# One ring of five buffers for k's results, in place of a ring of three and one of two

## The chip, the cores and the metric

The kernel runs on one core of a Trainium2 chip. The metric is the device time of one execution in microseconds (us), as the median of several runs. Of a profiled execution, the trace gives the times of all instructions from the start of its span.

## The reference

Two branches read the same `x` (2048 tokens, width 640, float32) and are mixed by a gate per token. Branch `a` is linear attention with 32 heads of 20, branch `b` a gated unit with 1536 inner columns.

```
phi = lambda t: jnp.where(t > 0, t + 1, jnp.exp(t)) + 1e-6
q, k, v = split(x @ wqkv)                       # per head
pq, pk = phi(q), phi(k)
kv = einsum("bhsd,bhse->bhde", pk, v)           # sum over tokens
z  = einsum("bhsd->bhd", pk)                    # sum of phi(k) over tokens
o  = (pq @ kv) / (pq . z + 1e-6)
a  = o @ wo
b  = (sigmoid(x @ w_gate) * (x @ w_up)) @ w_down
g  = sigmoid((x * gate_w).sum(-1, keepdims=True))
out = g * a + (1 - g) * b
```

The change touches only the part that computes `phi(k)` and `z`.

## The kernel before

All products are float32, each split into a high and a low part and made of three matmuls (`mm3`, lines 406 to 408). In the first stage (about the first 140 us) the kernel makes `phi(k)` for all tokens and at once multiplies it with the tokens' rows of `x`, into `gt`. The other stages (queries, the gated unit, the output) follow and do not use the tiles of this change.

The tokens stand in 16 tiles of 128. A block `b` (0 to 7) is a pair of token tiles, side 0 from one half of the tokens and side 1 from the other. Four chunks of two blocks each are worked off. Blocks 0 and 1 (`KPlain`) use plain products. Blocks 2 to 7 (`KBlock`) use a scheme with fewer products: seven of them (`s1` to `s7`), of which sums and differences, formed ahead on VectorE (DVE), are the operands. For each chunk the steps of both its blocks alternate: `s1` of a, `s1` of b, ... `s5` of b, and then `s6`, `s7`, `sum_b` and `phi` of each. Between these products PE works on `GTBatch` parts, the products of `phi(k)` and `x` of earlier blocks.

A block has two results of 640 columns (and two columns for the gate):

- side 0 is finished by `phi_a`: ScalarE (ACT) applies Exp and Relu to sums in `ta` and PSUM, the Relu parts go to a new tile `kr` (320 columns used, 320 wide), and DVE combines them.
- side 1 is collected in a tile `kb` (two halves of 322 columns), which `s3` allocates and ACT and DVE fill in `s3`, `s5` and `sum_b`; `phi_b` then works in place. In `KPlain`, `phi_b` allocates `kb` itself.

Either result `r` then has two readers. `z_add(r)` issues a DMA on GpSimd's (POOL's) queue that adds the tile to `zacc` (`accum_op`); each such DMA writes all of `zacc`. `k_split` (ACT and DVE) makes the high and the low part, `pkh` and `pkl`. Only when all these have read the tile can its buffer be given to a later tile of the same ring; the wait for that stands at the later tile's first writer. Rings are made by the tile pool `p1`, by tag: tag `kr` has three buffers, tag `kb` two.

The order of instructions is written out by the kernel's own planner (`Order`). It keeps a clock for PE, ACT and DVE, and puts queued work (splits of `x`, sums, weight splits) between the fixed steps wherever by these clocks it fits (`fill`, `_fits`). `place` finds, for a tile, the tile that had its buffer before, by the tag's number of buffers, and `data` takes the end of that tile's last use into account. `Ring` and `Rings` do the same for the two DMA queues, with the contiguous run of both sides of a transfer (`Ring.run`) as a term of its length. On the chip each engine runs its instructions in the order written, and waits by semaphores.

PE's products accumulate in PSUM tiles `ch`, `dd`, `cc` and `rot`. A block's `s3`, `s5` and `s6` all go to its `ch`: `s5` may start only when ACT has copied `s3`'s sum from `ch` to `kb[:, 0]`, and `s6` when ACT has copied `s5`'s to `kb[:, 1]`.

Of the kernel before, what the change touches and what calls it, by code (L numbers as in the profile page):

```python
# [7 lines left out]
F32 = mybir.dt.float32  # L8
# [6 lines left out]
P = 128  # L15
# [6 lines left out]
HALF = D // 2  # L22
HW = HALF + 2
# [350 lines left out]
def gated_mix_kernel(ctx: ExitStack, tc: tile.TileContext, xt, xn, wk, wv, wo, wst_q, wst_f, out_t):  # L374
# [38 lines left out]
    def prod(out, terms, first):  # L413
        for n, t in enumerate(terms):
            mm3(out, *t, first and n == 0, n == len(terms) - 1)

    def act(out, src, fn, after="", **kw):
        order.on_act(width(out), after, out, src)
        nc.scalar.activation(out, src, fn, **kw)  # L419
# [5 lines left out]
    def vec3(out, a, scalar, b, op0, op1, after=""):  # L425
        order.on_vec(width(out), after, 1.0, out, a, b)
        nc.vector.scalar_tensor_tensor(out, a, scalar, b, op0=op0, op1=op1)
# [57 lines left out]
    p1 = p1_cm.__enter__()  # L485
# [291 lines left out]
    def tok(b, side):  # L777

        pr, j = divmod(b, 4)
        return (2 * pr + side) * 4 + j  # L780
# [18 lines left out]
    def phi(dst, lo_src, hi_src, i):  # L799

        e = m1.tile([P, 2, HALF], F32, name="ke", tag="ma", bufs=2)
        act(e[:, 0], lo_src[:, :HALF], AF.Exp, "pv")
        act(e[:, 1], hi_src[:, :HALF], AF.Exp)
        act(dst[:, 0], lo_src[:, :HALF], AF.Relu)
        act(dst[:, 1], hi_src[:, :HALF], AF.Relu)
        vec_copy(logit[:, i:i + 1], lo_src[:, HALF:HALF + 1])
        vec3(dst, e, 1.0, dst, OP.min, OP.add, "a")
        KR[i] = dst
        z_add(dst)

    def vec_copy(out, src, after=""):
        order.on_vec(width(out), after, 1.0, out, src)
        nc.vector.tensor_copy(out, src)

    def kr_tile():
        return p1.tile([P, 2, HALF], F32, name="kr", tag="kr", bufs=3)

    class KBlock:
        def __init__(self, b):
# [23 lines left out]

        def s3(self):
            order.need(("pk", self.b - 2))
            self.kb = p1.tile([P, 2, HW], F32, name="kb", tag="kb", bufs=2)
            prod(self.ch[:, :HW], self.xt(1, ksh[:, 1], ksl[:, 1]), False)
            act(self.kb[:, 0], self.ch[:, :HW], AF.Copy, "p")

# [21 lines left out]
            add(self.kb[:, 0], self.cc[:, :HW], self.kb[:, 0], "p")  # L871

        def phi_a(self):
            phi(kr_tile(), self.ta, self.ch, tok(self.b, 0))

        def phi_b(self):
            i = tok(self.b, 1)
            e = m1.tile([P, 2, HALF], F32, name="ke", tag="ma", bufs=2)
            k = self.kb[:, :, :HALF]
            act(e, k, AF.Exp, "pv")  # L880
            vec_copy(logit[:, i:i + 1], self.kb[:, 0, HALF:HALF + 1])
            act(k, k, AF.Relu)
            vec3(k, e, 1.0, k, OP.min, OP.add, "a")
            KR[i] = k
            z_add(k)

    class KPlain:
# [15 lines left out]
                    mm3(self.ps[s][h][:, :HW], *x, *k_half(k, h), k == 0, k == KC - 1)  # L903

        def phi_a(self):
            phi(kr_tile(), *self.ps[0], tok(self.b, 0))

        def phi_b(self):
            kb = p1.tile([P, 2, HW], F32, name="kb", tag="kb", bufs=2)
            phi(kb[:, :, :HALF], *self.ps[1], tok(self.b, 1))  # L910

    def k_split(i, after=""):
# [14 lines left out]
    def z_add(r):  # L927

        gp.dma_start(zacc.rearrange(view2, j=2), r, accum_op=OP.add if z_started else OP.bypass)
        z_started.append(1)  # L930
# [1675 lines left out]
```

## Time and profile before

| | us |
|---|---|
| median of 3 runs | 732.84 (732.79 to 733.18) |
| the profiled execution | 732.54 |
| its span, first to last instruction | 730.6 |
| PE busy in the span | 724.0 |
| DVE busy | 563.7 |
| ACT busy | 360.1 |
| POOL busy | 94.7 |

A row of a timeline gives the start, the duration, the engine, the line of the program, the operation, and out<-in by the names of the tiles; a bracket at its end gives the idle time of the engine before it and what ended it. Most instructions come from helpers, so that many share a line (L419 is ACT's helper, L423 that of DVE for two tensors, L363 the one that issues DMAs); they are told apart by their tiles. "PE ch L406 <- ACT kb" reads: a matmul into `ch` waited for an ACT instruction on `kb`.

### The profile page before, as it was taken

The page shows a single profiled execution, that of the slowest core. Times are in us where ns is not written, and L with a number is a line of the kernel's source. Part 1 is how long each engine was busy: PE and PEld are TensorE (multiplying, and loading weights), DVE is VectorE, ACT ScalarE, POOL GpSimd, SP SyncE. Part 2 cuts the span into 40 slices and gives each one's busy share as a digit, 9 for nine tenths or more (in the row PEclk, how much of TensorE's full clock was granted, in tenths as well). Part 3 has the DMA queues.
Part 4 walks back from the last instruction along what each step waited for, and adds up shares of the span by engine and source line. Part 5 has one row for each costly group of instructions (what it writes and reads, how often), then busy time and mean ns, then how long its engine had stood idle before and what let it go on. Part 6 is the DMA issues. An engine that isn't in the chain of part 4 may idle for free.

```text
span 730.6 us, 10105 instructions
## 1 busy us (share of the span) xinstructions
PE 724.0 (99%) x3569; PEld 622.0 (85%) x3569; DVE 563.7 (77%) x989; ACT 360.1 (49%) x668; POOL 94.7 (13%) x161
## 2 busy tenths in 40 slices
PE   9989999999999999999999999999999999999997
PEld 8989999988888888888888888888888888888886
DVE  6878787987777889898989973457585867698783
ACT  6864648357556653535455363454333232334550
POOL 0211111113221211111210032001000041000000
PEclk9999999999999999999999999999999999999999
DMA  7655648698787866457687389879889697859212
GB/s 248 168 166 118 186 108 243 152 347 295 273 296 258 330 241 237 185 212 256 255 324 265 106 295 333 310 247 316 253 286 340 211 326 213 298 217 340 83 62 102
DMA packets 71945, 173.54 MB, mean 238 GB/s; under 512 B 11690, under 2 KB 33466, under 8 KB 68310
## 3 DMA queue, kind: packets, MB, share of 16 engines
q1 hardware_dynamic: 55526, 109.99, 46.2%
q0 software_dynamic: 16224, 62.74, 24.2%
q8 instruction: 28, 0.46, 0.2%
q14 instruction: 23, 0.19, 0.1%
q10 hardware_dynamic: 144, 0.16, 0.1%
HBM read 103.96 MB, written 63.92 MB: 230 GB/s over the span
## 4 chain that ended last, share of the span: by engine, by line
PE 98%; DMA 1%; DVE 1%; ACT 0%; issue 0%; ACTq 0%
PE ch L406 11%; PE ch L408 10%; PE ch L407 10%; PE cc L408 9%; PE cc L406 9%; PE cc L407 9%; PE dd L406 7%; PE dd L408 7%; PE dd L407 7%; PE rot L408 6%; PE rot L407 6%; PE rot L406 6%; PE rot L1505 1%; DMA zacc<-kb 1%; PE rot L494 0%; PE ch L980 0%
## 5 line engine op out<-in xcount | busy, mean ns | idle before, releaser
L419 ACT ACTIVATE c<-ch 128x512 f32<-128x512 f32 x52 | 31.1, 598 | 96.4 <-PE ch L408 96.2
L423 DVE TENSOR_TENSOR hf<-c,hf 128x512 fp32r<-128x512 f32 x75 | 51.1, 686 | 24.7 <-ACT hf L419 24.5
L419 ACT ACTIVATE hf<-c 128x512 fp32r<-128x512 f32 x75 | 46.0, 624 | 28.0 <-DVE c L423 28.0
L423 DVE TENSOR_TENSOR c<-cc,c 128x512 f32<-128x512 f32 x40 | 27.6, 689 | 37.6 <-PE cc L408 24.3
L406 PE MATMUL ch<-xth,ws 128*128 128x512 f32 x112 | 43.7, 390 | 0.0
L407 PE MATMUL ch<-xtl,ws 128*128 128x512 f32 x112 | 43.6, 389 | 0.0
L408 PE MATMUL ch<-xth,ws 128*128 128x512 f32 x112 | 43.6, 389 | 0.0
L423 DVE TENSOR_TENSOR tb<-rot,tb 128x512 f32<-128x512 f32 (+1 forms) x61 | 39.2, 672 | 3.0 <-PE rot L408 3.0
L423 DVE TENSOR_TENSOR tb<-dd,tb 128x512 f32<-128x512 f32 x44 | 30.1, 685 | 9.7 <-PE dd L408 9.6
L406 PE MATMUL dd<-xrh,wg 128*128 128x512 f32 x90 | 35.2, 391 | 0.0
L408 PE MATMUL dd<-xrh,wg 128*128 128x512 f32 x90 | 35.0, 389 | 0.0
L407 PE MATMUL dd<-xrl,wg 128*128 128x512 f32 x90 | 35.0, 389 | 0.0
L419 ACT ACTIVATE c<-dd 128x512 f32<-128x512 f32 x22 | 13.1, 598 | 44.2 <-PE dd L408 44.2
L423 DVE TENSOR_TENSOR c<-c,c 128x512 f32<-128x512 f32 x46 | 31.6, 686 | 2.6 <-ACT c L419 2.0
L406 PE MATMUL cc<-xbh,ws 128*128 128x512 f32 x84 | 32.7, 389 | 0.0
L407 PE MATMUL cc<-xbl,ws 128*128 128x512 f32 x84 | 32.7, 389 | 0.0
L408 PE MATMUL cc<-xbh,ws 128*128 128x512 f32 x84 | 32.7, 389 | 0.0
L419 ACT ACTIVATE dd<-ch 128x512 f32<-128x512 f32 x22 | 12.8, 582 | 33.6 <-PE ch L408 33.6
L423 DVE TENSOR_TENSOR wst<-wst 128x256 f32<-128x256 f32 (+2 forms) x69 | 27.4, 412 | 1.4
L408 PEld LDWEIGHTS ch<-xth,ws 128*128 128x128 f32 x112 | 21.0, 188 | 4.7 <-DVE ws L423 0.3
L407 PEld LDWEIGHTS ch<-xtl,ws 128*128 128x128 f32 x112 | 21.0, 188 | 4.3
L406 PEld LDWEIGHTS ch<-xth,ws 128*128 128x128 f32 x112 | 21.0, 188 | 4.1
(643 smaller groups left out, 2349.8 us busy)
## 6 DMA issues: line engine op xcount, KB each, us to landing
wf<-ws POOLq DMA_DIRECT2D x12, 1152.0 KB, 7.7
ws<-wf SPq DMA_DIRECT2D x11, 1152.0 KB, 8.1
wst<-wst_f SPq DMA_DIRECT2D x12, 640.0 KB, 5.2
wf<-wg POOLq DMA_DIRECT2D x12, 640.0 KB, 6.2
wd<-wd POOLq DMA_DIRECT2D x12, 640.0 KB, 8.1
wg<-wf SPq DMA_DIRECT2D x12, 640.0 KB, 5.3
wf<-wd SPq DMA_DIRECT2D x10, 640.0 KB, 9.2
xnst<-xn SPq DMA_DIRECT2D x16, 320.0 KB, 4.3
```

Source lines behind the costliest of these rows:

```text
L406: nc.tensor.matmul(out, l_hi, r_hi, start=first, stop=False, skip_group_check=True)
L407: nc.tensor.matmul(out, l_hi, r_lo, start=False, stop=False, skip_group_check=True)
L408: nc.tensor.matmul(out, l_lo, r_hi, start=False, stop=last, skip_group_check=True)
L419: nc.scalar.activation(out, src, fn, **kw)
L423: nc.vector.tensor_tensor(out, a, b, op=op)
L1505: nc.tensor.matmul(ps[:w, :w], v[:, m, :w], gt[:, m, c0:c0 + w], start=(m == 0), stop=(m == KC - 1))
```

## The change

`kr_tile` now makes tiles of the width of `kb` under one tag with five buffers, and `kb` tiles are made by it too. `phi_a` uses 320 of the 322 columns of each half, so that a `kr` tile is no longer one contiguous row in its partition.

```
-    def kr_tile():
-        return p1.tile([P, 2, HALF], F32, name="kr", tag="kr", bufs=3)
+    def kr_tile(name="kr"):
+        return p1.tile([P, 2, HW], F32, name=name, tag="kr", bufs=5)
...
     # KBlock.s3
-            self.kb = p1.tile([P, 2, HW], F32, name="kb", tag="kb", bufs=2)
+            self.kb = kr_tile("kb")
...
     # KBlock.phi_a
-            phi(kr_tile(), self.ta, self.ch, tok(self.b, 0))
+            phi(kr_tile()[:, :, :HALF], self.ta, self.ch, tok(self.b, 0))
...
     # KPlain.phi_a
-            phi(kr_tile(), *self.ps[0], tok(self.b, 0))
+            phi(kr_tile()[:, :, :HALF], *self.ps[0], tok(self.b, 0))
...
     # KPlain.phi_b
-            kb = p1.tile([P, 2, HW], F32, name="kb", tag="kb", bufs=2)
+            kb = kr_tile("kb")
             phi(kb[:, :, :HALF], *self.ps[1], tok(self.b, 1))
```

## The prediction

> **What bounds the kernel now.** I read the page first, for the busy shares and the chain that ended last.
>
> ```profile
> span 730.6 us, 10105 instructions
> PE 724.0 (99%) x3569; PEld 622.0 (85%) x3569; DVE 563.7 (77%) x989; ACT 360.1 (49%) x668; POOL 94.7 (13%) x161
> PE 98%; DMA 1%; DVE 1%; ACT 0%; issue 0%; ACTq 0%
> PE ch L406 11%; PE ch L408 10%; PE ch L407 10%; PE cc L408 9%; PE cc L406 9%; PE cc L407 9%; PE dd L406 7%; PE dd L408 7%; PE dd L407 7%; PE rot L408 6%; PE rot L407 6%; PE rot L406 6%; PE rot L1505 1%; DMA zacc<-kb 1%; PE rot L494 0%; PE ch L980 0%
> ```
>
> PE is the bound: 98% of the chain is matmuls. A change of buffers can only move the remaining 2%. In that rest one entry is not compute: `DMA zacc<-kb`, the accumulation into `zacc` that reads a `kb` tile, which is a tile of this change. So the next view is who PE waited for, over the whole span.
>
> ```profile
> PE ch L406 <- ACT kb L419: 2.0, 2, 1.2
> PE rot L494 <- PEq L2597: 0.8, 1, 0.8
> ```
>
> That is all of it: 0.8 us at the warm-up, and two waits of 2.0 us together for ACT writing `kb`. Where they are, the table by stretches shows.
>
> ```profile
> 36.00:41.00 5.00, 5.00 (x36) 5.00 (x34) 4.46 (x10) 1.17 (x3) 1.21 (x1) 1.00 0.34 53
> 41.00:45.00 4.00, 1.99 (x12) 1.47 (x12) 2.00 (x5) 3.00 (x8) 0.00 (x0) 1.00 0.11 17
> 45.00:49.00 4.00, 4.00 (x29) 4.00 (x29) 4.00 (x8) 3.62 (x8) 0.00 (x0) 1.00 0.95 295
> ```
>
> The first busy column after the length is PE. Before 41 us and after 45 us it is full; between them it has 1.99 of 4.00 us, 12 matmuls in place of 29. This is the first block pair that uses the transformed products (blocks 2 and 3). The reason is in ACT's timeline and in the chain of waits (its row for the DMA follows here last).
>
> ```profile
> 37.17 0.62 ACT L419 ACTIVATE xth<-xst 128x512 fp32r<-128x512 f32 x1
> 42.00 0.44 ACT L419 ACTIVATE kb<-ch 128x322 f32<-128x322 f32 x1 [4.20 <-DMA zacc<-kb]
> 42.34 0.62 ACT L419 ACTIVATE xth<-xst 128x512 fp32r<-128x512 f32 x1
> 42.86 0.46 ACT L419 ACTIVATE ksh<-xnl 128x322 fp32r<-128x322 f32 x1
> 43.58 0.46 ACT L419 ACTIVATE k5h<-pkl 128x322 fp32r<-128x322 f32 x1
> 43.95 0.76 ACT L419 ACTIVATE kb<-ch 128x322 f32<-128x322 f32 x2
> ...
> 37.77 4.13 DMA zacc<-kb
> ```
>
> At 42.00 ACT evicts block 3's product into its new `kb` tile. The ring has two `kb` buffers; block 3 gets the one of block 1, which the accumulation issued at 37.77 still reads until 41.90. ACT stands still for 4.20 us, and behind it are queued the split of `xth`, the weight splits and the next two evictions.
>
> **The change part by part.** (1) The wait goes. In the order of allocation (`kr0 kb0 kr1 kb1 kb2 kb3 kr2 kr3 kb4 kb5 kr4 kr5 ...`) `kb3` is the sixth tile, so in a ring of five it takes the buffer of `kr0`; it is also the first buffer given back. Its accumulation is long over:
>
> ```profile
> 18.89 0.68 POOL L363 DMA_DIRECT2D zacc<-kr  x1 [18.37 <-DVE logit L813]
> 23.23 1.26 POOL L363 DMA_DIRECT2D zacc<-kb  x1 [3.67 <-DVE logit L813]
> ```
>
> Each accumulation waits for the one before it to land, since all write `zacc`; so `kr0` is free at 23.23 at the latest, 14 us before ACT wants it. What the wait costs PE:
>
> ```profile
> 37.53 0.30 PE L406 MATMUL cc<-ksh,xth 128*128 128x322 f32 x1
> 40.96 0.30 PE L408 MATMUL ch<-ksh,xtl 128*128 128x322 f32 x1
> 42.50 0.41 PE L406 MATMUL ch<-ksh,xth 128*128 128x322 f32 x1 [1.23 <-ACT kb L419]
> 43.33 0.31 PE L408 MATMUL ch<-ksh,xtl 128*128 128x322 f32 x1
> 44.42 0.42 PE L406 MATMUL ch<-k2h,xth 128*128 128x322 f32 x1 [0.78 <-ACT kb L419]
> 44.83 0.30 PE L408 MATMUL ch<-k2h,xtl 128*128 128x322 f32 x1
> ```
>
> From 37.53 to 40.96 PE starts 24 matmuls, 23 steps of 3.43 / 23 = 0.149 us. From 40.96 to 44.83 it makes 9 steps (six of block 3's `s5`, then three of block 2's `s6`), which undisturbed are 9 x 0.149 = 1.34 us and took 3.87. Lost: 2.53 us. That is more than the 2.0 of the waits view, because the first matmul after each gap also takes 0.41 and 0.42 instead of 0.30.
>
> (2) Is something else late there? With the wait gone, ACT evicts `kb3` at 37.8 (end of `xth` at 37.79). The second gap (0.78) comes from ACT's queue: block 2's next eviction stands behind `xth` and three weight splits, whose inputs DVE makes:
>
> ```profile
> 38.56 0.68 DVE L423 TENSOR_TENSOR xst<-xst 128x512 f32<-128x512 f32 x1
> 39.98 0.49 DVE L423 TENSOR_TENSOR pkl<-pkl 128x322 f32<-128x322 f32 x1
> 43.00 0.69 DVE L423 TENSOR_TENSOR xtl<-xst,xth 128x512 fp32r<-128x512 f32 x1 [2.53 <-ACT xth L419]
> 44.82 0.88 DVE L423 TENSOR_TENSOR kb<-cc,kb 128x322 f32<-128x322 f32 x2
> ```
>
> `xth` can start when its sum ends, 38.56 + 0.68 = 39.24; with ACT's own steps (0.52 to the first `ksh`) the last split `k5h` waits for its sum, 39.98 + 0.49 = 40.47, and runs to about 40.9. Block 2's eviction then needs PE's `s5`, which ends at 40.96 + 0.30 = 41.26; it runs to 41.7. PE reaches `s6` at 40.96 + 7 x 0.149 = 42.00. So this gap closes too, with 0.3 us to spare. On DVE the stretch from `xtl` to the two `kb` sums (1.82 us from 43.00 to 44.82) moves to begin at 40.47; the first sum ends near 42.8, and `s7`, which needs it, starts at 42.00 + 9 x 0.149 = 43.34: 0.5 us to spare. If my chain through ACT is wrong by more than these 0.3, the second gap stays (0.78 and its slow matmul, 44.42 - 43.33 - 0.15 = 0.94): gain 2.53 - 0.94 = 1.59. Ends: 1.59 and 2.53; I take 2.53, since every step of the upper one has its row.
>
> (3) The other rings. Every later tile now also takes a buffer with another history. By allocation five back, the tightest are `kr4` after `kb3` and `kr6` after `kb5`:
>
> ```profile
> 64.58 1.18 POOL L363 DMA_DIRECT2D zacc<-kb  x1 [3.58 <-DVE xst L423]
> 97.08 1.19 POOL L363 DMA_DIRECT2D zacc<-kb  x1 [3.32 <-DVE xst L423]
> 80.60 0.47 ACT L419 ACTIVATE kr<-ta 128x320 f32<-128x320 f32 x1
> 114.40 0.46 ACT L419 ACTIVATE kr<-ta 128x320 f32<-128x320 f32 x1
> ```
>
> With the slowest landing of a `kb` accumulation (8.0, below) they are free at 72.6 and 105.1, 8 and 9 us before they are written. No new wait: 0.
>
> (4) `kr` tiles become as wide as `kb` tiles, and only 320 of 322 columns are used, so their accumulation reads two runs per partition instead of one. The `kb` tiles have that form already, so their rows price it.
>
> ```profile
> L363 POOL DMA_DIRECT2D zacc<-kr x8: 678/888/922, 18.9 to 132.0; - x8
> DMA to landing us min/median/max: 3.6/4.1/8.6
> L363 POOL DMA_DIRECT2D zacc<-kb x8: 1183/1192/1265, 23.2 to 136.1; - x8
> DMA to landing us min/median/max: 4.1/4.4/8.0
> L432 DVE TENSOR_SCALAR zperm<-zacc x1: 814/814/814, 180.3 to 180.3; 128x640 f32<-128x640 f32 x1
> ```
>
> Each of eight `kr` accumulations costs POOL 1.19 instead of 0.89 us and lands 0.3 later by the medians. What hides it: with the ring wait gone, the next reader of `zacc` is the copy at 180.3, over 40 us behind the last issue at 136.1. Taken at 0; if the chain of accumulations stood on the path, 8 x 0.30 = 2.4 us.
>
> The Trainium skill speaks against this edit: its page "Perfetto Trace Analysis", section "Contiguity and DMAs", says that for DMA it is contiguity within a partition line that matters, and wants layouts to keep it; here a contiguous 640 becomes 320 + 320. The rows agree in sign, with 0.30 us of POOL and 0.3 of landing; by the rule alone the time would not fall, by the rows the loss is behind a 40 us cover.
>
> (5) The order of instructions comes from the planner, which knows the rings (it looks up a tile's predecessor by the number of buffers) and the run lengths. In its own clocks no ring wait of `kr` or `kb` binds, before or with the new predecessors, so these lookups change nothing. The shorter run makes its `kr` transfers a little longer and their share of the engines smaller; worked through by its formulas this moves a store of `qp` by some hundredths of a us, less than the closest of the decisions that follow it. I take the order as unchanged.
>
> Sum: 2.53 + 0 + 0 + 0. From 44.83 on PE has no further wait in the view, so all that follows moves forward by the same amount. The profiled execution took 732.54 us (span 730.6 and 1.9 around it) and becomes 730.0. It lies 0.3 below the median of the runs (732.84), so for the median I say 730.3. A measurement of this kernel can tell 0.2%, 1.5 us, from no change.
>
> **Rivals.** (a) The wait goes and another takes part of its place: ACT's or DVE's queue is late at `s6` or `s7`. For it: spare time of only 0.3 and 0.5 us; against: each input has its row. Gain 1.0 to 1.6, so 731.2 to 731.8. 10%, half of it beyond 0.2%.
>
> (b) The longer `kr` accumulations stand on a path after all: 2.53 - 2.4 leaves 0.1, 732.7. Against: 8 us of margin at the tightest buffer and 40 at `zacc`. 3%. The contiguity rule of the Trainium skill ("Perfetto Trace Analysis", "Contiguity and DMAs") points this way.
>
> (c) The change does not do what it says: `kb3` gets a buffer whose accumulation is as late as now. For it: only that the pool, not the kernel, picks the buffer; against: at that point four of the five are either unused or returned earlier. 732.8, 3%.
>
> (d) Slower: the planner's order does change somewhere in chunks 2 and 3, and an ACT instruction is put in front of an eviction that PE needs. It decides once that instruction (0.44 to 0.62 us by the rows of ACT) is longer than the eviction's lead over PE, about 0.3 us at `s6`. Price, from the nearest rows: a gap such as the one here, 2.53; one in each of the two later chunks gives 730.3 + 5.06 = 735.4. Against: (5). 8%.
>
> **How the numbers follow.** The forecast has 76%, alone from 729.8 to 731.1. Taking in (a) up to its weaker end and the uncertainty of the runs, the range is 729.8 to 732.2; (b), (c) and (d), 14%, are mostly outside. Faster by over 0.2%: 76 + 5 = 81%. Within 0.2%: 5 + 3 + 3 = 11%. Slower: 8%.
>
> **What would show it.** Right: PE's waits have no entry for ACT `kb`; ACT evicts `kb` twice within about 1 us near 37 to 38; PE is full between 41 and 45 us; `zacc<-kb` leaves the chain; POOL's issue for `kr` is near 1.19 us; instruction counts are unchanged and DVE's `zperm` starts near 177.8. Wrong in step 2: a PE wait at 42 to 43 us with ACT or DVE as releaser. Wrong in step 3: an ACT wait for `zacc<-kr` or `zacc<-kb` at 70 to 120. Wrong in step 5: other instructions next to each other on ACT and DVE, and new waits of PE after 45 us.

## The result, and the profile after

| | before | changed |
|---|---|---|
| median, us (9 runs each) | 732.22 (730.82 to 733.18) | 730.48 (730.01 to 730.97) |
| the profiled execution | 732.54 | 730.48 |
| its span | 730.6 | 728.6 |

The ratio is 0.9976, with a 95% interval of 0.9966 to 0.9986: faster by 0.24%, between 0.14 and 0.34%. The forecast, 730.3 us, is 0.2 off the measured median; as a change it was 2.53 us, or 0.35%, and the measured 1.74 us between the medians is less. Why it is less is the question of the experiments.

First the page of the changed kernel (busy times, and the chain of work that ended last by engine), and who PE waited for.

```profile
span 728.6 us, 10106 instructions
PE 724.0 (99%) x3569; PEld 622.6 (85%) x3569; DVE 564.0 (77%) x989; ACT 360.1 (49%) x668; POOL 97.0 (13%) x161
PE 99%; DVE 0%; issue 0%
...
PE rot L494 <- PEq L2597: 0.8, 1, 0.8
```

PE's waits for ACT `kb` are gone, and so is the DMA in the chain; only the warm-up's 0.8 us is left. The same stretches as before (length, PE, PEld, DVE, ACT, POOL, clock, DMA, GB/s):

```profile
36.00:41.00 5.00, 5.00 (x36) 5.00 (x35) 5.00 (x11) 3.27 (x9) 1.19 (x1) 1.00 0.31 48
41.00:45.00 4.00, 4.00 (x29) 4.00 (x28) 3.87 (x8) 3.25 (x8) 0.00 (x0) 1.00 0.71 209
45.00:49.00 4.00, 4.00 (x29) 4.00 (x28) 3.27 (x8) 3.56 (x8) 1.18 (x1) 1.00 0.99 349
```

PE is full from 41 to 45 us. ACT's timeline shows what it does in place of standing still:

```profile
37.27 0.44 ACT L419 ACTIVATE kb<-ch 128x322 f32<-128x322 f32 x1 [0.63 <-PE ch L408]
37.60 0.62 ACT L419 ACTIVATE xth<-xst 128x512 fp32r<-128x512 f32 x1
38.16 0.44 ACT L419 ACTIVATE kb<-ch 128x322 f32<-128x322 f32 x1
39.71 0.63 ACT L419 ACTIVATE xth<-xst 128x512 fp32r<-128x512 f32 x1 [1.11 <-DVE xst L423]
40.97 0.46 ACT L419 ACTIVATE k5h<-pkl 128x322 fp32r<-128x322 f32 x1
41.73 0.44 ACT L419 ACTIVATE kb<-ch 128x322 f32<-128x322 f32 x1 [0.30 <-PE ch L408]
42.62 0.44 ACT L419 ACTIVATE kb<-ch 128x322 f32<-128x322 f32 x1 [0.45 <-PE ch L408]
```

And PE's, at the same matmuls:

```profile
37.96 0.30 PE L406 MATMUL cc<-ksh,xth 128*128 128x322 f32 x1
42.42 0.31 PE L406 MATMUL ch<-k2h,xth 128*128 128x322 f32 x1
```

From the first matmul of block 2's `s4` to the first of its `s6` it is 42.42 - 37.96 = 4.46 us; before it was 44.42 - 37.53 = 6.89. That is 2.43 us, and with the slow first matmul of `s6` (0.42 against 0.31) the 2.53 of the forecast. In this execution everything already starts 0.43 us later (37.96 against 37.53), which is why the span falls by only 2.0. The delay arises before 12 us (48 matmuls from 4 to 12 us, 51 in the first profile of before); the other profiles of before have 47 to 51 there, so such a delay comes without the change too.

### The profile page after: what moved, and what is told of

The parts are those of the page before. It is cut to its first block, busy times and chain, and to the rows that moved or that the text cites. A ratio compares the mean times of both kernels' runs of the same rounds, so it can differ in the third digit from the quotient of the medians.

```text
span 728.6 us, 10106 instructions
## 1 busy us (share of the span) xinstructions
PE 724.0 (99%) x3569; PEld 622.6 (85%) x3569; DVE 564.0 (77%) x989; ACT 360.1 (49%) x668; POOL 97.0 (13%) x161
## 4 chain that ended last, share of the span: by engine, by line
PE 99%; DVE 0%; issue 0%
PE ch L406 11%; PE ch L407 11%; PE ch L408 11%; PE cc L407 9%; PE cc L408 9%; PE cc L406 9%; PE dd L407 8%; PE dd L408 8%; PE dd L406 8%; PE rot L407 6%; PE rot L408 6%; PE rot L406 6%; PE rot L1505 1%; PE rot L494 0%; PE ch L980 0%; PE dd L980 0%
```

## The experiments

Theory 1: the whole gain is ACT's wait for the buffer, and the two-run form of `kr` costs nothing. Theory 2: the wait was worth 2.5 us in every execution and the form gives 0.8 back. Theory 3, from the spread of the times of before (730.8 to 733.2, against 730.0 to 731.0 after): the wait has a different length in each execution.

**Three `kb` buffers, the rings apart.**

```
-  ... name="kr", tag="kr", bufs=3)          # contiguous, as before
+  ... name="kr", tag="kr", bufs=2)
-  ... name="kb", tag="kb", bufs=2)
+  ... name="kb", tag="kb", bufs=3)
```

> The rings stay apart, with two buffers for kr and three for kb in place of three and two; kr tiles keep one contiguous row. Theory 1 (the whole gain is ACT's wait for the kb buffer): PE's wait for ACT kb is gone from the waits and the time falls as with the shared ring, ratio to before about 0.9976. Theory 2 (the wait was worth 2.5 us in every run and the two-run form of kr gives 0.8 us of it back): the ratio is about 0.9965, since kr is contiguous here.

Median 730.43 us, ratio 0.9973 (0.9960 to 0.9986). PE has no wait for ACT `kb`. The time is that of the shared ring though `kr` is contiguous. This fits theory 1, and sharing as such is not needed; by theory 2 the median would be some 0.8 us lower. The ratio alone cannot tell the two apart.

**Only the form of `kr`.**

```
-  return p1.tile([P, 2, HALF], F32, name="kr", tag="kr", bufs=3)
+  return p1.tile([P, 2, HW], F32, name="kr", tag="kr", bufs=3)[:, :, :HALF]
```

> Only the form: kr tiles are 2 x 322 wide and 320 of each half are used, the rings stay three and two. The wait of block 3 for its kb buffer stays. Theory 1: the form costs PE nothing by itself, but two kr accumulations before that of block 1 each issue 0.3 us longer, so the wait may grow by up to 0.6 us: ratio 1.000 to 1.001. Theory 2: the form also costs elsewhere, 0.8 us or more: ratio 1.001 to 1.002.

Ratio 1.0002 (0.9988 to 1.0015): no change that can be seen, though the interval would still hide about 1 us. POOL's issue has its price and nobody waits for it; ACT's wait is even shorter than in the first profile of before, 3.84 against 4.20 us:

```profile
41.84 0.44 ACT L419 ACTIVATE kb<-ch 128x322 f32<-128x322 f32 x1 [3.84 <-DMA zacc<-kb]
L363 POOL DMA_DIRECT2D zacc<-kr x8: 861/1183/1221, 18.9 to 133.5; - x8
```

**The ring of five with contiguous `kr` rows**, timed twice.

```
-  return p1.tile([P, 2, HW], F32, name=name, tag="kr", bufs=5)
+  t = p1.tile([P, 2 * HW], F32, name=name, tag="kr", bufs=5)
+  return (t if name == "kb" else t[:, :D]).rearrange(view2, j=2)
...
-  phi(kr_tile()[:, :, :HALF], ...)
+  phi(kr_tile(), ...)
```

> The shared ring of five, but a kr tile uses the first 640 columns of its buffer as one row, so its accumulation reads one run per partition as before. Theory 1: the time is that of the changed kernel, ratio to before about 0.9976, with POOL's issue for kr back at 0.89 us. Theory 2: 0.8 us faster than the changed kernel, ratio about 0.9965.

> The shared ring of five with contiguous kr rows, timed again beside before on another chip or at another time. By theory 3 its own times stay within 730.0 to 731.2 as before, while the ratio to before depends on how many of before's executions have the long wait: between 0.995 and 0.999. By theory 2 (the two-run form of kr costs 0.8 us) its median is 0.8 us below the 730.48 us of the changed kernel.

Medians 730.21 and 730.55 us (730.03 to 731.15 and 730.04 to 731.04), ratios 0.9968 (0.9955 to 0.9982) and 0.9976 (0.9965 to 0.9988), with POOL's issue for `kr` at 0.89 us again. The kernel's own times are those of the changed kernel in both, so the form costs nothing that shows and theory 2, with its 0.8 us, has fallen. The ratio moves while these times stay: it is before that differs from one time to the next. This is not a matter of different chips: on one and the same chip the median of before was 732.83 us beside the first four kernels here, and 731.15 beside the three that follow.

**A shared ring of four.**

```
-  ... tag="kr", bufs=5)
+  ... tag="kr", bufs=4)
```

> The shared ring with four buffers, one fewer in all than before. By allocation order block 3's kb then takes the buffer of block 0's kb, whose accumulation lands near 32 us, 6 us before ACT writes; later buffers are free 5 us or more ahead (kb of block 5 after that of block 3: 69 against 74 us). Theory 1 (which buffer is taken counts, not how many there are): no wait, the same time as with five, ratio about 0.9976. The rival (the number of buffers counts): a wait comes back at block 5 or at block 3, ratio 0.998 to 1.002.

Median 730.51 us, ratio 0.9965 (0.9953 to 0.9977), no wait for `kb` on PE. One buffer fewer than before in all, and the same gain: what counts is whose buffer is taken.

**The suspected accumulation twice**, in the kernel before and in the changed one.

```
   z_started.append(1)
+  if len(z_started) == 4:     # block 1's kb
+      nc.gpsimd.dma_start(zacc.rearrange(view2, j=2), r, accum_op=OP.add)
```

> The kernel before, with the accumulation of block 1's kb issued twice in a row (its share counts twice in z), the planner not told. The second one holds the kb buffer for another issue to issue of about 4.3 us. Theory 1 (PE loses what ACT waits for the buffer beyond some 1.7 us): PE loses 4 to 4.5 us more between 36 and 49 us, ratio to before about 1.006. The rival (the accumulation is only named in the chain, something else holds ACT): no change.

> The changed kernel with the same doubled accumulation of block 1's kb. Its buffer goes to block 4's kb, which ACT writes near 71 us. Theory 1: no wait, the time of the changed kernel, ratio to before about 0.997. The rival (the accumulation chain bears on the time in other ways too): up to 4 us slower than the changed kernel, ratio up to 1.002.

Before: median 736.81 us of four runs (734.85 to 738.24), ratio 1.0077 (1.0052 to 1.0101). Changed: 730.21, ratio 0.9980 (0.9966 to 0.9995), no wait for `kb` on PE. So it is this DMA that holds ACT and PE, and with the shared ring even twice of it does not. All four executions of the doubled kernel before have a mean granted clock of 0.994 to 0.998, so that a part of their loss is the half clock described below. ACT and POOL of the doubled kernel before:

```profile
44.08 0.44 ACT L419 ACTIVATE kb<-ch 128x322 f32<-128x322 f32 x1 [6.12 <-DMA zacc<-kb]
35.49 1.20 POOL L363 DMA_DIRECT2D zacc<-kb  x1 [3.61 <-DVE xtl L423]
39.91 1.17 POOL L930 DMA_DIRECT2D zacc<-kb  x1 [3.21 <-DMA zacc<-kb]
```

The wait grew by less than a whole DMA, because here the first of the two was issued at 35.49, not at 37.77 as in the first profile.

**One link of the chain of accumulations left out** (block 0's `kb`; z lacks its share), in the kernel before.

```
   # z_add: for the second tile alone no DMA is issued; the planner is told as before
-  gp.dma_start(...)
+  if len(z_started) != 1: gp.dma_start(...)
```

> The kernel before without the accumulation of block 0's kb (z lacks its share), the rings untouched. The chain of accumulations is then one link shorter: block 1's kb is issued near 28 to 30 us and lands 4 to 5 us before ACT wants its buffer. Theory 1: no wait of PE for ACT kb, the time of the changed kernel, ratio to before about 0.997. The rival (two kb buffers are too few in any case): the wait stays.

PE has no wait for `kb`, with two `kb` buffers as before, and the median is 730.53 us (730.00 to 731.56). The ratio, 0.9990 (0.9979 to 1.0001), is no proof, since 11 of the 19 executions of before in this comparison were themselves below 731.4. The times of POOL were expected wrongly: the next accumulation, issued at 24.77, still took until 32.82. In both kernels the slow link is the one in flight when SyncE issues its last load of `xnst` and that of `qraw`, near 23 to 24 us; that these loads slow it is argued, not shown, since it is the second link in both. The bracket at 32.82 names `ksl`, but that DMA had landed at 32.3 (7.5 us after its issue), and in all 14 profiles the accumulation of block 1's `kb` is issued 0.5 to 0.6 us after the one before it has landed. ACT's eviction of block 3 at 38.32 waits for nothing all the same:

```profile
24.77 0.93 POOL L363 DMA_DIRECT2D zacc<-kr  x1 [2.70 <-DVE logit L813]
32.82 1.22 POOL L363 DMA_DIRECT2D zacc<-kb  x1 [7.12 <-DVE ksl L423]
38.32 0.44 ACT L419 ACTIVATE kb<-ch 128x322 f32<-128x322 f32 x1
```

**The kernel before, unchanged, for four more profiles.**

> The kernel before, unchanged, for a second profile. Theory 3 (the wait has a different length in each execution, since the landing of the accumulations before it varies, and the medians show its mean): ACT's wait differs from the 4.20 us of the first profile, and the execution's time differs by what PE loses, time = about 730.3 plus the loss. The rival (the wait is 4.2 us in all executions, and the spread of the times is from elsewhere): the same wait, whatever the time.

> As for the second profile of the kernel before: by theory 3 ACT's wait has yet another length, and time = about 730.3 plus what PE loses by it; by the rival the wait is 4.2 us again.

> As for the second profile of the kernel before: by theory 3 ACT's wait has yet another length, and time = about 730.3 plus what PE loses by it; by the rival the wait is 4.2 us again.

> The kernel before, unchanged, once more. By theory 3, PE's loss is ACT's wait less 1.77 us, and times near 730.5 are executions in which the accumulation of block 1's kb is issued near 35.5 us instead of 37.7: the wait is then about 2 us and PE loses 0.2 at most. Times near 733 go with a wait near 4 us, times over 734 with a wait near 4 us and a stretch of half clock after 44 us.

The table has ACT's wait, PE's loss (from the first matmul of `s4` to that of `s6`, less the undisturbed 4.46 us), and the time, for these, the first profile and two of the kernels above.

| execution | wait | loss | time |
|---|---|---|---|
| before, first profile | 4.20 | 2.43 | 732.54 |
| before, second | 3.93 | 2.16 | 733.07 |
| before, third | 4.09 | 2.32 | 733.22 |
| before, fourth | 3.95 | 2.18 | 734.11 |
| before, fifth | 3.46 | 1.68 | 732.06 |
| only the form of `kr` | 3.84 | 2.07 | 734.06 |
| accumulation twice | 6.12 | 4.34 | 735.88 |

Loss = wait - 1.77 holds in all seven within 0.01 us: the first 1.8 us of ACT's wait are covered, each further one costs PE as much. Outside this stretch the profiles are nearly alike: in all 14, of any kernel, the first matmul of `s4` starts at 37.4 to 38.2 us, and from the first matmul of block 3's `s6` to the end of the span it is 683.4 to 683.7 us (684.2 in the third of before). The length of the wait does vary, as theory 3 has it, but among these five of before only by 0.7 us. The fourth has the same loss as the second and is 1 us longer. Its table by stretches shows why (length, PE, clock, DMA, GB/s):

```profile
44.00:46.00 2.00, 1.68 (x8) 0.74 0.43 147
46.00:48.00 2.00, 2.00 (x9) 0.50 1.00 318
48.00:50.00 2.00, 2.00 (x14) 0.91 1.04 366
...
42.39 0.42 PE L406 MATMUL ch<-ksh,xth 128*128 128x322 f32 x1 [0.98 <-ACT kb L419]
44.32 0.42 PE L406 MATMUL ch<-k2h,xth 128*128 128x322 f32 x1 [0.77 <-ACT kb L419]
44.72 0.31 PE L408 MATMUL ch<-k2h,xtl 128*128 128x322 f32 x1
46.41 0.47 PE L406 MATMUL cc<-ksh,xbh 128*128 128x322 f32 x1
48.63 0.31 PE L406 MATMUL ch<-k2h,xth 128*128 128x322 f32 x1
```

After the two gaps PE is granted half its clock for about 3.4 us (some 44.9 to 48.4): nine matmuls in 46 to 48 us where the full clock does fifteen or sixteen, each of 0.47 instead of 0.31 us. From 44.72 to 48.63 it makes 16 steps, 3.91 us for 16 x 0.149 = 2.38: another 1.53 us. With 2.18 and 0.1 for the slow first matmul that is 3.8, and 734.1 - 3.8 = 730.3, the time of the changed kernel. The execution with only the form of `kr` at 734.06 and the doubled one show the same stretch of 0.50; the other four of before do not, though the second has almost the same gaps (0.96 and 0.78 us).

So a profiled execution of before pays about 1.8 to 2.5 us, or about 3.8; by their times, others seem to pay little or nothing. Beside the kernels above 71 executions of before were timed: 25 below 731.4 us, 35 from 731.6 to 733.9, and 11 from 734.0 up; the mean granted clock is 0.996 to 0.998 in ten of these 11 and 0.999 or 1.000 in all others. Of the 77 executions of the kernels without the wait none is below 0.999, and 74 lie below 731.2 us. By the rule of the table, the first group would be executions in which the accumulation of block 1 lands some 2 us earlier. It was issued at 35.10 and 35.68 us in two profiles of ring kernels (five with rows, four) and at 35.49 in the doubled one, against 37.17 to 38.16 in the five of before and 37.56 to 38.00 in the other profiles in which all links run. The kernel does not decide this: the ring of five with rows has a profile of either sort. Its POOL, in the first profile and in the second, to set beside the 31.76 and 37.77 of before:

```profile
30.71 0.92 POOL L363 DMA_DIRECT2D zacc<-kr  x1 [6.15 <-DVE xst L423]
35.10 1.20 POOL L363 DMA_DIRECT2D zacc<-kb  x1 [3.47 <-DVE xtl L423]
...
32.29 0.92 POOL L363 DMA_DIRECT2D zacc<-kr  x1 [7.05 <-DVE ksl L423]
37.56 1.20 POOL L363 DMA_DIRECT2D zacc<-kb  x1 [4.34 <-DVE ksl L423]
```

From this link to the next issue it is 4.4 us in the first, 5.3 in the second and 6.0 in the first profile of before. In the three profiles that issue it before 31 us it lands after 3.8 to 4.3 us, in the ten that issue it between 31.7 and 33.0 after 4.6 to 5.5; why was not found. But no profile of before fell into the early group, so that this cause of the times below 731.4 is argued, not shown.

## Why the prediction was right, and where it was off

- **Step 1, the wait goes:** right, in its place and with all rows. The changed kernel's `kb3` takes a buffer whose DMA landed long ago, as do the rings of four and of three `kb`. The term's size, 2.53 us, was read off one execution and taken for the kernel's. It was right for that execution; in the profiles the wait's cost goes from 1.8 to 3.8 us, by the times alone down to nothing, and the difference of the medians was 1.74 us here. This is the term that was mis-sized. The three executions known to the prediction, 732.79 to 733.18, showed no such spread; the six after them went from 730.82 to 732.97 and took the median of before from 732.84 to 732.22. The time itself was forecast within 0.2 us, since its base, 732.84, by its executions' times also held the wait, so that base less loss was about the time without it.
- **The half clock** was in no step. The forecast took the matmuls after the gap at full clock, since the first profile shows 1.00 there. In the one execution above 734 us that has a profile it adds 1.53 us. The Trainium skill ("TensorE: Matmul & The Clock Gate", "What's actually happening") has TensorE's clock fall to half after an idle window of some 3.4 us, by an activity window that runs freely. The trace agrees in the 3.4 us of half clock, and nearly the same gaps bring it in one execution and not in another, as with a window that runs freely. It differs in what it takes: two gaps, 0.98 and 0.77 us, with six matmuls between them.
- **Step 2, nothing else is late:** right. The chain through ACT came as worked out, moved by the 0.43 us of the late start: `k5h` at 40.97 (40.5 forecast), the eviction at 41.73 (41.3), `s6` at 42.42 (42.00). The spare 0.3 and 0.5 us held, and rival (a) did not come.
- **Step 3, the other buffers:** right; no ACT wait for `zacc` is left, even with four buffers.
- **Step 4, the form of `kr`:** right at 0. POOL pays what was forecast, eight issues of 1.18 us, and the DMAs land no later by the medians than 0.1 us:

```profile
L363 POOL DMA_DIRECT2D zacc<-kr x8: 863/1182/1221, 19.1 to 130.1; - x8
DMA to landing us min/median/max: 3.3/4.2/9.3
L432 DVE TENSOR_SCALAR zperm<-zacc x1: 817/817/817, 178.2 to 178.2; 128x640 f32<-128x640 f32 x1
```

  Rival (b) fell with the kernels of contiguous rows, which are no faster. The split row costs POOL 0.29 us an issue (0.89 to 1.18) and weighs nothing where no one waits for it.
- **Step 5, the order:** right. The instructions of PE, ACT, DVE and POOL stand in the same order in both profiles, so rival (d) did not come up. (The one instruction more in the page's total is a semaphore wait on SyncE.)

No version tried beats the changed kernel clearly: its median is 730.48, those of the other kernels without the wait lie from 730.21 to 730.55, within each other's spread.

## What to carry to other kernels

A ring is held by its slowest reader; where that is a chain of DMAs, ask whose buffer the waiting tile gets, and a shared ring, in the order of allocation, can hand it an older one at hardly any more memory (here 3220 columns in place of 3208; the ring of four takes less than before). Before a wait seen in one profile is entered as a gain, look at the spread of the times: where an unchanged kernel spreads over 2 us and more, the wait may be absent in some executions and dearer in others, and the gain in the median is a mixture. A short stall of PE can also be followed by a stretch at half clock that costs as much again.

## What was not expected of the hardware

Two gaps of PE of 0.98 and 0.77 us, 1.9 us apart, were followed by about 3.4 us of half clock in one of five profiles of the same kernel, at 1.53 us; gaps of 0.96 and 0.78 in another were not. An accumulating DMA of 320 KB that lands in 4.1 to 4.4 us by the medians of the two kernels took 7.5 to 9.3 us when it was in flight beside the loads near 23 us, and the next one, with hardly a transfer beside it, between 3.8 and 5.5 us in different executions. Chained by their common destination, these two set when the buffer was free.
